# Block-sparse attention and an expert layer on one core: another order of the tiles, and whole rows' scores in quarters of TensorE

## The chip, the core and the metric

The kernel runs on one core of a Trainium2 chip. The metric is the time of one execution on the device, in microseconds (us). Each core has TensorE (PE, matrix products into PSUM), VectorE (DVE), ScalarE (ACT), GpSimd (POOL), and SyncE (SP), which here only issues transfers. Transfers (DMA) are also issued from POOL's queue. Every engine works through its own instructions in the order in which they were written out, and waits for others by semaphores.

## The reference

Attention over 4 batches, 8 heads, 768 positions and head size 64, in blocks of 32 positions, followed by an expert layer on the 3072 tokens:

```python
scores = scale * np.matmul(q, k.transpose(0, 1, 3, 2))
mask = np.abs(blk_i - blk_j) <= window                      # window = 1
mask = mask | (blk_i == 0) | (blk_j == 0) | (blk_i == n_blocks - 1) | (blk_j == n_blocks - 1)
for qb in range(n_blocks):                                  # 24 blocks, 3 sampled keys blocks each
    for kb in sampled_blocks[qb]:
        mask[qb * block:(qb + 1) * block, kb * block:(kb + 1) * block] = True
scores = np.where(mask, scores, -1000000000.0)
attn = exp(scores - max); attn = attn / (sum(attn) + 1e-09)
x = (attn @ v), heads side by side: [3072, 512]
h = np.maximum(x @ w_in, 0.0)                               # [512, 2048]
out = h * h @ w_out                                         # [2048, 512]
```

So a row of an inner block attends to at most eight blocks: the first and the last one, three around itself and three sampled ones. The rows of the first and the last block of a batch attend to all 24 blocks; these are called whole rows.

## The kernel before, in words

**Tiles and chunks.** A tile is 128 positions (4 blocks) of one batch; there are 6 per batch and 24 in all. `order` (line 163) lists them as tile 0 to 5 of batch 0, then of batch 1, and so on. Three tiles make a chunk (`UC`), so there are 8 chunks and two per batch. The attention of a chunk is done ahead of its expert pass. `moe(c)` (line 842) is the expert pass of chunk c: it turns the three tiles' outputs on PE (`turn`, line 765, tile `xt`, split into a high and a low part `xh`, `xl`), then goes through 16 blocks of the hidden layer, each with 12 products (`hidden`, `ph`, line 788) and, two blocks later, its products with the output weights (`project`, `po`, lines 816 and 826).

**Half tiles.** The class `Half` does the inner rows of one tile for four heads. Scores go to two PSUM banks in pieces of 64 rows by 32 columns of PE's array, eight places at once (line 374). The maxima are taken by DVE, the exps by ACT, the transposes by PE in the first two chunks (`turn`, line 437) and by ACT moves and a DVE transpose later (`turn_blocks`), and then come the values (line 459) and the division (`norm`).

**Whole rows.** The class `Whole` does one pair of heads of a batch. The queries of both heads, of the first and of the last block lie in one 128 x 128 operand `QG`, padded with zeros, so that one product with 128 rows and 128 columns gives the scores of both heads against 16 blocks, and a second one against 8 (line 546). Two banks hold them. There are four such units per batch. The first batch's exps are turned on PE (line 584), the others' by moves and a DVE transpose. In `units` (line 629) the whole rows belong to the even chunks (`wholes = [] if c % 2 else ...`): chunk 0 starts with four of them, and then its six half tiles follow.

**Order of the work.** The class `Stream` writes the order out: each unit is a generator, started at a set step and resumed after the lags in `LAG`, `LAG_1` (chunk 1) and `LAG_0` (chunk 0). Before the first expert pass only attention runs (the first stage); from then on each step of an expert pass, 96 to a pass, lets one step of the attention of the next chunk go in between. The score tiles of both kinds and `ph` share five PSUM banks (`SBUFS`), and three more hold the sums of `po`, and in the first stage the turned exps and the values.

**Loads in the first stage.** Keys `kn` and, for whole rows, the values of a batch in natural order (`vn`) come on POOL's queue. On SP's queue come `QG`, q, the static V blocks (first and last), the window V blocks of tile 0 (line 304), and the sampled V blocks: for each of the three tiles 12 transfers with an address from a register (line 317). Windows of tiles 1 and 2 are copied from `vn` by POOL, ACT and DVE (`copy_window`, line 217), the static blocks by ACT (`copy_static`, line 209). Sampled keys are copied by POOL (`copy_keys`, line 263), the fixed keys by POOL (line 284). The weights come as 64-bit numbers on POOL's queue and are cut to 32 bits by ACT and DVE (`cut`, lines 708 to 720); `cut_next` does one step of that, and in the first stage it is called from step 30 on, every 5 steps. Weight blocks named in `SINGLE` are kept as one part and split in each pass (lines 754 and 755), the others are split once.

Of the kernel before, what the change touches and what calls it, by code (L numbers as in the profile page):

```python
# [2 lines left out]

# [53 lines left out]
SINGLE = (1, 2, 3, 5, 6, 7, 9, 10, 11, 12, 13, 14, 15)  # L57
# [21 lines left out]
MOVES_0 = 22  # L79


FIXED_0 = 7
ON_ACT = 12
KEYS_N = 2
# [3 lines left out]
WO_LOW = 3  # L88
# [8 lines left out]
def tile_block_sparse_attention_moe(ctx: ExitStack, tc, kd, knd, qd, qgd, vd, vnd, samp, const, wcat, out):  # L97
# [27 lines left out]
    def indices():  # L125

        n = NBLK * NRAND
        si = rot.tile([1, 2 * n], I32, tag="r", name="si", bufs=2)
        nc.sync.dma_start(si, samp)
        rows = rot.tile([1, 6 * n], F32, tag="ct", name="rows", bufs=2)  # L130
# [25 lines left out]
    QG = one.tile([P, NPAIR, P], F32, name="QG")  # L156
# [6 lines left out]
    order = [(b, t) for b in range(B) for t in range(NT)]  # L163
# [47 lines left out]
    def copy_window(k, i, j, n, copy):  # L211

        b, t = order[k]
        blk = centre(NJ * t + j) - 1 + n
        assert 0 < blk < NBLK - 1
        r = blk % NJ * BLK
        copy(V[k][1][(1 + n) * BLK : (2 + n) * BLK, i, j], st["vn", b, i][r : r + BLK, blk // NJ])

    def load_vn(b, hf, eng=nc.sync, own=None):

        vn = (own or rot).tile([P, NT, HW // 2], F32, tag="vn", name=f"vn{b}_{hf}", bufs=1)
        eng.dma_start(vn.rearrange("p t c -> p (t c)"), vnd[b, hf])
        st["vn", b, hf] = vn
# [15 lines left out]
    def load_q(b, t, eng=nc.sync, own=None):  # L239
        q = (own or rot).tile([P, NJ, NPAIR, BLK], F32, tag="q", name=f"q{b}_{t}", bufs=1 if own else 2)  # L240
        n = NJ * NPAIR * BLK
        eng.dma_start(q.rearrange("p a b c -> p (a b c)"), qd[b, :, t * n : (t + 1) * n])
        st["q", b, t] = q
# [9 lines left out]
    def copy_keys(b, t, own=None):  # L253

        vals = sampled(t, 0, POOL)
        kg = keys_of(b, t, own)
        for u in range(2):
            if t < UC:
                static_keys(b, t, u, nc.gpsimd.tensor_copy)
# [20 lines left out]
    def static_keys(b, t, u, copy=nc.scalar.copy):  # L280
# [3 lines left out]
        copy(dst, src.broadcast_to(list(dst.shape)))  # L284

# [38 lines left out]
    class Half:  # L324
# [34 lines left out]
        def scores(self):  # L359
            b, t, u = self.b, self.t, self.u  # L360
            q, kg, kn = st["q", b, t], st["kg", b, t], st["kn", b, u]
            self.sb = [bank(f"s{self.name}_{e}") for e in range(2)]
# [35 lines left out]
        def next_keys(self):  # L398

            b, t = order[min(self.k + self.u, len(order) - 1)]  # L400
            if b > 0 and t < 2:
# [79 lines left out]
        def loads(self, step):  # L481

            k = order.index((self.b, self.t))
            if step == 0 and self.t == NT - 1 and self.b + 1 < B:
                eng = nc.gpsimd if self.b == 0 else nc.sync
                load_keys(self.b + 1, self.u, eng)
                if self.u == 0:
                    load_whole(self.b + 1, eng)
                    load_vn(self.b + 1, 0, eng)
# [11 lines left out]
            if step == 2 and k not in range(1, UC) and n < len(order):  # L501
                if self.t == NT - 1:
                    load_static(n, self.u)
# [3 lines left out]
    class Whole:  # L507
# [4 lines left out]
        def __init__(self, b, pr):  # L512
            self.b, self.pr = b, pr
            self.name = f"{b}_{pr}"

        def run(self, bank, lag):
            self.scores()
            yield lag["s"]
            self.maxima()
            yield lag["x"]  # L520
            self.exps()
            yield lag["t"]
            if self.b > 0:
                yield from self.move()
                yield lag["w0"]
                self.turn_blocks()
                yield lag["w"]
            else:
                pt = self.turn(bank)
                yield lag["c"]  # L530
                self.copies(pt)
                yield lag["v0"]
            po = self.values(bank)
            if self.pr == 1 and self.b > 0:
                load_vn(self.b, 1)
# [470 lines left out]
```

## Time and profile before

| what | value |
|---|---|
| time, median of the runs | 759.31 us |
| lowest and highest run | 759.08 and 762.59 us |
| the profiled execution, its time | 760.55 us |
| the profiled execution, its span | 758.8 us |
| mean granted clock of TensorE | 0.992 |
| PE, ACT, POOL, DVE busy | 97%, 71%, 66%, 66% |
| transferred | 97.45 MB, mean 128 GB/s |

The span goes from the first to the last instruction; the time also holds what lies around it. The slices of the page divide the span into 40 equal parts and give each engine's busy share in tenths. In the groups each row is a line of the kernel, an engine and an operation; "xh,wi 128*128 128x384" means an array form of 128 rows by 128 columns and a moving operand of 384 columns. A 32-bit product that isn't of the rounded kind is recorded as two instructions, so the scores of one old unit are "x4". In a timeline row come the start, the length, engine, line, operation, the tiles (out<-in), the shape, the count and, in brackets, how long the engine stood idle before it and for whom.

### The profile page before, as it was taken

The numbers are of one execution on the slowest core, as the hardware profiler recorded it, in microseconds if no ns is written. First come the engines' busy times: TensorE is split into PE (matmuls) and PEld (weight loads), VectorE is DVE, ScalarE is ACT, GpSimd is POOL, SyncE is SP. The second block draws the span as 40 slices with busy tenths as digits, with TensorE's granted clock in tenths as the row PEclk, the third lists the DMA queues.
The fourth block names the chain that finished last, engine by engine and source line by source line (L and its number), as shares of the span: only waits on it lengthen the run. The fifth ranks groups of instructions, "written<-read, shape, count | busy, mean of one in ns | idle before, by whom it ended". The sixth has DMA issues, their size and how long they took to land.

```text
span 758.8 us, 26292 instructions
## 1 busy us (share of the span) xinstructions
PE 732.4 (97%) x9832; PEld 612.3 (81%) x9832; DVE 499.8 (66%) x987; ACT 539.7 (71%) x1193; POOL 502.3 (66%) x636
## 2 busy tenths in 40 slices
PE   4879999999999999999999999999999999999997
PEld 2656776668888888888888888887888888888986
DVE  5785785658785756667777575666868666645452
ACT  5896877798876876789786767679876776733222
POOL 6963844227776675757767567666876575777885
PEclk9799999999999999999999999999999999999999
DMA  8776799544543536544434344655344352201001
GB/s 283 224 215 172 228 264 344 130 117 131 140 114 93 146 86 176 153 109 128 113 105 106 101 126 109 221 120 140 79 124 118 75 143 64 51 1 44 1 1 41
DMA packets 92290, 97.45 MB, mean 128 GB/s; under 512 B 14787, under 2 KB 79428, under 8 KB 92164
## 3 DMA queue, kind: packets, MB, share of 16 engines
q1 hardware_dynamic: 86036, 72.41, 37.1%
q0 software_dynamic: 5696, 22.58, 9.2%
q8 instruction: 78, 1.28, 0.7%
q10 hardware_dynamic: 432, 0.79, 0.3%
q14 instruction: 48, 0.39, 0.2%
HBM read 89.43 MB, written 6.29 MB: 126 GB/s over the span
## 4 chain that ended last, share of the span: by engine, by line
PE 85%; ACT 5%; DMA 4%; DVE 4%; issue 1%; SPq 1%; ACTq 0%; POOL 0%; DVEq 0%; POOLq 0%
PE ph L788 33%; PE po L826 30%; PE s L374 7%; PE pv L459 5%; PE po L816 4%; PE g L546 2%; PE pvg L604 2%; DMA V<-in_v_dram 2%; DMA KG<-in_k_dram 1%; PE xt L773 1%; PE pt L437 1%; DVE xl L777 1%; ACT V L209 1%; DMA kn<-in_kn_dram 1%; SPq L317 1%
## 5 line engine op out<-in xcount | busy, mean ns | idle before, releaser
L413 ACT ACTIVATE pm<-p 32x256 f32<-32x256 f32 x576 | 239.2, 415 | 13.2 <-DVE p L391 4.8
L788 PE MATMUL ph<-xh,wi 128*128 128x384 f32 x832 | 237.8, 347 | 0.0
L826 PE MATMUL po<-wo,gh 128*128 128x512 f32 x672 | 213.8, 399 | 0.0
L755 POOL TENSOR_TENSOR wi<-W,wi 128x512 fp32r<-128x512 f32 x104 | 142.3, 1368 | 68.4 <-DVE wi L754 35.2
L806 POOL TENSOR_TENSOR gl<-gf,gh 128x384 fp32r<-128x384 f32 x112 | 117.4, 1048 | 93.0 <-DVE gf L804 80.6
L755 POOL TENSOR_TENSOR wo<-WO,wo 128x512 fp32r<-128x512 f32 x112 | 145.9, 1302 | 49.5 <-DVE wo L754 48.5
L792 ACT ACTIVATE r<-ph 128x384 f32<-128x384 f32 x128 | 63.0, 492 | 161.3 <-PE ph L788 156.1
L804 DVE SCALAR_TENSOR_TENSOR gf<-ph,r 128x384 f32<-128x384 f32 x112 | 62.3, 556 | 150.3 <-ACT r L792 136.4
L788 PEld LDWEIGHTS ph<-xh,wi 128*128 128x128 f32 x832 | 150.4, 188 | 13.4 <-issue 7.4
L826 PEld LDWEIGHTS po<-wo,gh 128*128 128x128 f32 x672 | 123.5, 188 | 23.0 <-issue 2.8
L788 PE MATMUL ph<-xl,wi 128*128 128x384 f32 x416 | 141.4, 340 | 0.0
L826 PE MATMUL po<-wo,gl 128*128 128x512 f32 x336 | 133.2, 396 | 0.0
L754 DVE CAST wo<-WO 128x512 fp32r<-128x512 f32 x112 | 84.4, 753 | 0.0
L788 PEld LDWEIGHTS ph<-xl,wi 128*128 128x128 f32 x416 | 78.2, 188 | 6.9 <-issue 2.9
L826 PEld LDWEIGHTS po<-wo,gl 128*128 128x128 f32 x336 | 63.1, 188 | 15.7 <-POOL gl L806 1.0
L385 DVE TENSOR_REDUCE m<-s 128x2 f32<-128x512 f32 x96 | 61.6, 683 | 11.2 <-PE s L374 10.9
L799 ACT ACTIVATE gh<-r 128x384 fp32r<-128x384 f32 x112 | 59.0, 526 | 9.3 <-ACT r L792 0.4
L459 PEld LDWEIGHTS pv<-V,pT 128*32 128x32 f32 x3072 | 47.7, 110 | 19.8 <-issue 9.5
L459 PE MATMUL pv<-V,pT 128*32 128x65 f32 x3072 | 56.2, 223 | 5.0 <-ACT pT L446 4.8
L788 PE MATMUL ph<-xh,WI 128*128 128x384 f32 x192 | 54.4, 344 | 0.8 <-ACT xh L776 0.8
L374 PE MATMUL s<-KG,q 64*32 64x160 f32 x1536 | 51.2, 305 | 1.4 <-issue 1.0
L418 DVE STREAM_TRANSPOSE pT<-pm 128x1024 f32<-128x1024 f32 x36 | 44.6, 1239 | 4.9 <-ACT pm L413 4.7
(85 smaller groups left out, 933.0 us busy)
## 6 DMA issues: line engine op xcount, KB each, us to landing
craw<-in_w_dram POOLq DMA_DIRECT2D x32, 512.0 KB, 5.9
V<-in_v_dram SPq DMA_DIRECT2D x504, 32.5 KB, 1.8
KG<-in_k_dram SPq DMA_DIRECT2D x216, 64.0 KB, 2.0
V<-in_v_dram SPq DMA_DIRECT2D x28, 390.0 KB, 4.5
q<-in_q_dram SPq DMA_DIRECT2D x24, 256.0 KB, 3.0
out_dram<-ot SPq DMA_DIRECT2D x21, 256.0 KB, 2.5
V<-in_v_dram SPq DMA_DIRECT2D x16, 292.5 KB, 4.2
vn<-in_vn_dram SPq DMA_DIRECT2D x5, 780.0 KB, 6.4
```

What stands on the lines that cost most here:

```text
L374: nc.tensor.matmul(self.sb[e][j * BLK : (j + 1) * BLK, i * NSLOT + a : i * NSLOT + z], q[r, j, pr, :], k, start=True, stop=True,)
L385: nc.vector.tensor_reduce(m[:, e], self.sb[e].rearrange("p (i c) -> p i c", i=2), axis=AX, op=ALU.max)
L413: nc.scalar.activation(p[a * BLK : (a + 1) * BLK, j], x[j * BLK : (j + 1) * BLK, :, a], AF.Exp, scale=SCALE)
L459: nc.tensor.matmul(po[j * BLK : (j + 1) * BLK, h * VW : (h + 1) * VW], self.pT[:, j, 2 * e + i, c], v[:, self.u, j, hv : hv + VW], start=( ...
L754: nc.vector.tensor_copy(w[:, 0], src)
L755: nc.gpsimd.tensor_tensor(w[:, 1], src, w[:, 0], op=ALU.subtract)
L788: nc.tensor.matmul(ph[:, :TOK], w, x, start=(i == 0), stop=(i == len(steps) - 1))
L792: nc.scalar.activation(r, ph[:, :TOK], AF.Relu)
L799: nc.scalar.activation(gh, r, AF.Square)
L804: nc.vector.scalar_tensor_tensor(gf, ph[:, :TOK], 0.0, r, op0=ALU.max, op1=ALU.mult)
L806: nc.gpsimd.tensor_tensor(gl, gf, gh, op=ALU.subtract)
L826: nc.tensor.matmul(acc[c][u], g[:, at], w[:, k], start=(f == 0 and i == 0), stop=(f == NF - 1 and i == 2))
```

## The change

1. **Order.** `order` becomes tile 1, 2, 3, 4, 5, 0 of each batch. The blocks with whole rows lie in tiles 0 and 5, so both are now in the second chunk of a batch, and `units` gives the whole rows to the odd chunks. Chunk 0 has half tiles only; the whole rows of batch 0 come with chunk 1, whose attention lies in the first expert pass. Output rows are addressed by tile.
2. **Whole rows' scores.** `QG` loses its zeros and is half as large. A `Whole` now does two pairs of heads at once. For each of the two spans of keys it makes four products of 64 rows by 64 columns (two heads of a pair, two pairs), each in another quarter of the array. Each head of the pairs has its own rows object (`Rows`), with two banks, so a score step holds four. The rest (maxima, exps, turning, values, norm) is done for each `Rows` as it was for a unit before, with other lags, and the exps have buffers of their own (`pg`).
3. **First stage.** Windows of all three tiles are loaded, those of tiles 1 and 2 of the order on POOL's queue; `vn` and `QG` come last on SP; q of the second and third tile comes on POOL's queue. Static V copies go from ACT to DVE, fixed keys from POOL to ACT. The weight loads are issued between the key copies. Half tiles start every 4 steps, `cut_next` is called from step 13 on, every 7 steps, and the turning of each tile (`turn_tile`) is put into the stage as soon as the tile is done.
4. **Room.** Weight block 4 joins `SINGLE`, and three buffers become smaller or fewer.

The diff's core:

```diff
-SINGLE = (1, 2, 3, 5, 6, 7, 9, 10, 11, 12, 13, 14, 15)
+SINGLE = (1, 2, 3, 4, 5, 6, 7, 9, 10, 11, 12, 13, 14, 15)
-EARLY = 23
+EARLY = 21
-LAG = {"s": 0, "e": 4, "v": 11, "x": 4, "t": 4, "c": 0, "v0": 13, "w0": 4, "w": 16, "n": -1}
+LAG = {"s": 0, "e": 4, "v": 11, "x": 4, "t": 4, "c": 0, "v0": 13, "g": 0, "n": -1}
+LAG.update({("w0", 0): 0, ("w", 0): 16, ("w0", 1): 0, ("w", 1): 8})
-STEP_0 = 5
-STEP_1, FIRST_1 = 12, 0
-LAG_1 = {**LAG, "v": 10, "x": 3, "t": 6, "v0": 5, "n": 0}
-LAG_0 = {"s": 2, "x": 2, "t": 3, "c": 2, "v0": 2, "n": 2}
-CUT_0 = (30, 5)
+STEP_0 = 4
+STEP_1, FIRST_1 = 12, 2
+G_1 = 6
+TURN_0 = (16, 1)
+LOADS_0 = (0, 1, 4, 8, 12)
+OTHERS_0 = (3, 4, 5, 6, 16, 16)
+LAG_1 = {**LAG, "v": 10, "x": 2, "t": 7, "v0": 6, "g": 5, "n": 0}
+LAG_1.update({("w0", 0): 0, ("w", 0): 4, ("w0", 1): 3, ("w", 1): 4})
+LAG_0 = {"s": 1, "x": 2, "t": 2, "c": 1, "v0": 6, "n": 1}
+CUT_0 = (13, 7)
...
-    order = [(b, t) for b in range(B) for t in range(NT)]
+    order = [(b, t % NT) for b in range(B) for t in range(1, NT + 1)]
...
+    class Whole:
+        def __init__(self, b, u):
+            self.b, self.u = b, u
+            self.rows = [Rows(b, u, e) for e in range(2)]
+        def run(self, bank, lag):
+            self.scores()
+            yield lag["s"]
+            for r in self.rows:
+                r.maxima()
+            yield lag["x"]
+            for r in self.rows:
+                r.exps()
+            yield lag["g"]
+            if self.b > 0:
+                for r in self.rows:
+                    yield from r.move()
+            for e, r in enumerate(self.rows):
+                yield lag["w0", e]
+                if self.b > 0:
+                    r.turn_blocks()
+                else:
+                    pt = r.turn(bank)
+                    yield lag["c"]
+                    r.copies(pt)
+                yield lag["w", e]
+                po = r.values(bank)
...
+        def scores(self):
+            kn = st["kn", self.b, self.u]
...
+            for i, n in enumerate(Rows.n):
+                for r in self.rows:
+                    r.sg.append(bank(f"g{r.name}_{i}"))
+                for a in range(2):
+                    for r in self.rows:
+                        at = slice(r.e * D, (r.e + 1) * D)
+                        nc.tensor.matmul(
+                            r.sg[i][a * 2 * BLK : (a + 1) * 2 * BLK, :n],
+                            QG[at, 2 * self.u + a],
+                            kn[at, 16 * i : 16 * i + n // BLK, a, :],
...
-        wholes = [] if c % 2 else [Whole(c // 2, pr) for pr in range(NPAIR)]
+        wholes = [] if c % 2 == 0 else [Whole(c // 2, u) for u in range(2)]
...
+            both += [(2 * i * STEP_1 + FIRST_1 + G_1, u) for i, u in enumerate(wholes)]
...
-        both += [(at + i * STEP + G_AT, u) for i, u in enumerate(wholes)]
+        both += [(at + 2 * i * STEP + G_AT, u) for i, u in enumerate(wholes)]
...
     load_keys(0, 0, nc.gpsimd)
-    load_whole(0)
-    load_q(0, 0)
+    load_keys(0, 1, nc.gpsimd)
+    load_q(*order[0])
+    load_window(0, 0)
     load_static(0, 0)
...
     load_sampled(0, 0, nc.sync, SP)
+    load_q(*order[1], nc.gpsimd)
+    load_q(*order[2], nc.gpsimd, "x", 5)
+    others = [
+        lambda: load_window(1, 0, nc.gpsimd),
+        lambda: load_sampled(1, 0, nc.sync, SP),
+        lambda: load_window(2, 1, nc.gpsimd),
+        lambda: load_sampled(2, 1, nc.sync, SP),
+        lambda: load_whole(0),
+        lambda: load_vn(0, 0),
+    ]
+    for i, _ in enumerate(chain(copy_keys(*order[0]), copy_keys(*order[1]), copy_keys(*order[2], begin))):
+        for at, f in chain(zip(LOADS_0, [cut_next] * AHEAD), zip(OTHERS_0, others)):
+            if at == i:
+                f()
...
+    turns = [(2 * STEP_0 * i + STEP_0 + TURN_0[0], i) for i in range(UC)]
...
-            f(*at, nc.scalar.copy)
-        if now >= MOVES_0 and moves:
-            f, *at = moves.pop(0)
             f(*at, nc.vector.tensor_copy)
```

More of the change, by code (lines that the diff above doesn't have):

```diff
@@ L2 @@
 from contextlib import ExitStack, suppress
+from itertools import chain
 import numpy as np
@@ L154, in indices @@
         return idx
-    QG = one.tile([P, NPAIR, P], F32, name="QG")
+    QG = one.tile([P, NPAIR, 2 * BLK], F32, name="QG")
     V = {0: [one.tile([P, 2, NJ, HW // 2], F32, name=f"V{c}") for c in range(2)]}
@@ L209, in copy_static, with load_vn @@
         copy(dst, src.broadcast_to(list(dst.shape)))
[L211 to L221, printed above, removed]
+    def load_vn(b, hf, eng=nc.sync):
+        vn = rot.tile([P, NT, HW // 2], F32, tag="vn", name=f"vn{b}_{hf}", bufs=1)
         eng.dma_start(vn.rearrange("p t c -> p (t c)"), vnd[b, hf])
@@ L237, in sampled, with load_q @@
         )[1]
-    def load_q(b, t, eng=nc.sync, own=None):
-        q = (own or rot).tile([P, NJ, NPAIR, BLK], F32, tag="q", name=f"q{b}_{t}", bufs=1 if own else 2)
+    def load_q(b, t, eng=nc.sync, tag="q", bufs=2):
+        q = rot.tile([P, NJ, NPAIR, BLK], F32, tag=tag, name=f"q{b}_{t}", bufs=bufs)
         n = NJ * NPAIR * BLK
@@ L398, in next_keys @@
         def next_keys(self):
-            b, t = order[min(self.k + self.u, len(order) - 1)]
-            if b > 0 and t < 2:
+            k = min(self.k + self.u, len(order) - 1)
+            b, t = order[k]
+            if b > 0 and k % NT < 2:
                 static_keys(b, t, 1 - self.u)
@@ L483, in loads @@
             k = order.index((self.b, self.t))
-            if step == 0 and self.t == NT - 1 and self.b + 1 < B:
+            if step == 0 and self.t == order[-1][1] and self.b + 1 < B:
                 eng = nc.gpsimd if self.b == 0 else nc.sync
@@ L505, in loads, with __init__ @@
                 load_sampled(n, self.u, nc.sync, SP)
-    class Whole:
+    class Rows:
         n = (16 * BLK, 8 * BLK)
[L512 to L535, printed above, removed]
-            if lag["n"] >= 0:
-                yield lag["n"]
-            self.norm(po)
-        def scores(self):
-            b, pr = self.b, self.pr
-            kn = st["kn", b, pr // 2]
-            self.sg = [bank(f"g{self.name}_{i}") for i in range(2)]
-            for i, n in enumerate(self.n):
-                k0 = 16 * i
-                nc.tensor.matmul(
-                    self.sg[i][:, :n], QG[:, pr], kn[:, k0 : k0 + n // BLK, pr % 2, :], start=True, stop=True
-                )
+        def __init__(self, b, u, e):
+            self.b, self.u, self.e = b, u, e
+            self.name = f"{b}_{u}{e}"
         def maxima(self):
-            m = self.m = rot.tile([P, 2], F32, tag="mg", name=f"mg{self.name}", bufs=2)
+            m = self.m = rot.tile([P, 2], F32, tag="mg", name=f"mg{self.name}", bufs=4)
             for i, n in enumerate(self.n):
@@ L686, in whole_block @@
             return WO[f]
-        return W1[f] if f in SINGLE else rot.tile([P, DM], F32, tag="ct", name=f"ct{f}", bufs=2)
+        return W1[f] if f in SINGLE else rot.tile([P, DM], F32, tag="ct", name=f"ct{f}", bufs=1)
     def cut_load(f, part):
@@ L965 @@
     vn = np.concatenate([vb[:, V_STATIC : V_STATIC + 1], vb[:, 1 : NBLK - 1], vb[:, V_STATIC + 1 :]], axis=1)
[L968 to L971 removed]
+    qg = pairs(q).reshape(B, P, NBLK, NPAIR, BLK)[:, :, [0, NBLK - 1]].transpose(0, 1, 3, 2, 4)
     kp = pairs(k)
```

120 lines of the change are left out of this document (60 added, 60 removed).

## The prediction

> **What bounds the kernel now.** I read the page first: busy time, the slices and the chain that ended last.
>
> ```profile
> PE 732.4 (97%) x9832; PEld 612.3 (81%) x9832; DVE 499.8 (66%) x987; ACT 539.7 (71%) x1193; POOL 502.3 (66%) x636
> PE   4879999999999999999999999999999999999997
> PE 85%; ACT 5%; DMA 4%; DVE 4%; issue 1%; SPq 1%; ACTq 0%; POOL 0%; DVEq 0%; POOLq 0%
> ```
>
> TensorE (PE) is busy in 97% of the span, and outside the first three of the 40 slices (19 us each) it has no room. So a change can gain in two ways only: end the first stage earlier, or give PE less to do after it. The same stages by windows (columns: stretch, its length, busy of PE, weight loads, DVE, ACT, POOL, granted clock, DMA share, GB/s):
>
> ```profile
> 27.00:30.00 3.00, 0.96 (x35) 0.64 (x36) 2.84 (x9) 2.94 (x9) 2.88 (x10) 1.00 1.04 337
> 30.00:33.00 3.00, 2.43 (x21) 1.98 (x20) 2.79 (x10) 1.23 (x3) 3.00 (x16) 0.50 0.84 192
> 33.00:36.00 3.00, 3.00 (x105) 2.37 (x108) 1.99 (x7) 2.77 (x7) 3.00 (x15) 0.50 0.45 128
> 45.00:57.00 12.00, 8.81 (x318) 7.20 (x317) 9.98 (x21) 12.00 (x27) 8.70 (x26) 1.00 0.81 213
> 65.00:155.00 90.00, 88.61 (x1132) 61.71 (x1130) 61.64 (x104) 72.65 (x142) 43.33 (x69) 1.00 0.78 223
> 160.00:245.00 85.00, 85.00 (x1278) 70.72 (x1277) 62.84 (x131) 67.95 (x159) 59.52 (x66) 1.00 0.48 119
> ```
>
> The end of the first stage is bound by ScalarE (ACT: 12.00 of 12.00 us between 45 and 57), its middle by transfers (DMA share 1.04 at 27 to 30). After 65 us PE is the bound. The timeline of PE gives the places that the sum needs:
>
> ```profile
> 6.61 4.26 PE L546 MATMUL g<-kn,QG 128*128 128x512 f32 x8 [6.61 <-DMA kn<-in_kn_dram]
> 22.63 0.57 PE L374 MATMUL s<-kn,q 64*32 64x96 f32 x16
> 31.15 1.97 PE L437 MATMUL pt<-ident,p 128*128 128x128 f32 x8
> 50.06 1.09 PE L437 MATMUL pt<-ident,p 128*128 128x128 f32 x8
> 56.03 1.38 PE L459 MATMUL pv<-V,pT 128*32 128x65 f32 x64 [0.97 <-ACT pT L446]
> 57.34 1.53 PE L773 MATMUL xt<-ident,x 128*128 128x128 f32 x12
> 59.64 0.44 PE L788 MATMUL ph<-xh,WI 128*128 128x384 f32 x1 [0.78 <-ACT xh L776]
> 60.59 0.44 PE L788 MATMUL ph<-xl,WI 128*128 128x384 f32 x1 [0.50 <-DVE xl L777]
> 61.30 0.40 PE L374 MATMUL s<-kn,q 64*32 64x96 f32 x16
> 62.44 0.44 PE L788 MATMUL ph<-xl,WI 128*128 128x384 f32 x1
> ```
>
> Whole rows take PE from 6.61, the first half tile starts at 22.63, the last values end at 56.03 + 1.38 = 57.4, and the expert's matmuls run without a break from 62.44.
>
> **A. The first stage.** Gone from it: four whole units (scores, maxima, exps, transposes, values), 48 window copies, two cut steps. ACT also loses the six static copies (to DVE) and gets the six static key copies (from POOL). So ACT falls behind no longer; what is late next is the sampled V blocks. They are 36 transfers on SP's queue, before and after, and no value matmul of a tile starts until its 12 have landed:
>
> ```profile
> 3.57 2.22 SPq L304 DMA_DIRECT2D V<-in_v_dram  x4
> 8.21 25.50 SPq L317 DMA_DIRECT2D V<-in_v_dram  x24
> 22.31 5.90 SPq L317 DMA_DIRECT2D V<-in_v_dram  x8
> 33.77 0.58 SPq L242 DMA_DIRECT2D q<-in_q_dram  x1
> 35.36 10.22 SPq L317 DMA_DIRECT2D V<-in_v_dram  x12
> V<-in_v_dram SPq DMA_DIRECT2D x38, 65.0 KB, 4.9
> DMA to landing us min/median/max: 1.6/1.9/9.8
> ```
>
> Before, 24 took 25.50 us and the last 12 took 10.22, with 35.36 - 34.35 = 1.0 us of register loads between. Undisturbed, eight took 5.90, or 0.76 from one to the next (seven steps and one issue of some 0.57). After the change SP has two window transfers in front instead of four (half of 2.22) and one q load instead of two, so the first can go at about 7.2. From there the 36 end between 7.2 + 36 x 0.76 + 2 x 1.0 = 36.6 (all undisturbed, two register loads) and 7.2 + 25.5 + 10.2 + 1.0 = 43.9 (as before). Against the fast end: POOL's queue now carries two q tiles, four windows of 390 KB and five weight blocks in the same 25 us, where it had two vn tiles and the five blocks, and the DMA engines were full (share 1.04) already. I take 41.5, two thirds of the way to the old pace. Landing costs 1.9 (median of the run) to 4.9 (median of these in the first 75 us); I take 3.0, so the last block is there at 44.5. Then two value steps of 1.38 follow: 47.3. New here is that PE has nothing to do for some 6 us before them. In the trace a stretch with 0.96 of 3 us busy is followed by a granted clock of 0.50 up to 36 us, and the eight transposes take 1.97 there against 1.09 at 50.06, 1.8 times as long. At half clock the two value steps take 5.0 instead of 2.8. I take 1.0 of the 2.2 as lost: the last values end at 48.3, a gain of 57.4 - 48.3 = **9.1** (bounds 57.4 - 36.6 - 1.9 - 2.8 = 16.1 and 57.4 - 43.9 - 4.9 - 5.0 = 3.6).
>
> The Trainium skill, "TensorE: Matmul & The Clock Gate", part 1 (the HAM clock gate), says that an idle window of about 3.4 us puts the clock to half and that it takes as long of steady work to lift it. The 0.50 in two rows agrees. By this rule all 2.2 us would be lost, and the estimate would be 1.2 us later than mine.
>
> **B. Into the expert.** Eight of the 12 transposes xt move ahead of the last values; the last tile's four, one ACT copy and one subtraction stay behind them. Before, from 57.4 to 62.44 were 5.0 us, in which PE also did 1.14 us of scores (61.30 to 62.44) and some 0.7 of ph: 3.2 for the passage, with three tiles to copy. The first ph that waited for xh came 2.2 us after 57.4, the first that waited for xl 3.2. With one tile left I take 2.8, between the two. Gain **0.4** (bounds 0 and 1.0).
>
> **C. PE's work after that.** Whole rows of batch 0 now lie in the expert's first pass, where nothing covers them. The rows for their price, all with PE full:
>
> ```profile
> 24.83 0.87 PE L584 MATMUL ptg<-ident,pg 128*128 128x128 f32 x6
> 110.26 0.40 PE L374 MATMUL s<-kn,q 64*32 64x96 f32 x16
> 111.40 1.13 PE L816 MATMUL po<-WO,gp 128*128 128x512 f32 x2
> 181.30 0.89 PE L604 MATMUL pvg<-vn,pTg 128*32 128x65 f32 x48
> 182.12 0.62 PE L788 MATMUL ph<-xh,wi 128*128 128x384 f32 x2
> 182.58 0.34 PE L788 MATMUL ph<-xl,wi 128*128 128x384 f32 x1
> 192.32 1.45 PE L546 MATMUL g<-kn,QG 128*128 128x512 f32 x4
> 193.42 0.53 PE L788 MATMUL ph<-xl,wi 128*128 128x384 f32 x1
> 193.79 0.51 PE L788 MATMUL ph<-xh,wi 128*128 128x384 f32 x2
> ```
>
> A ph matmul passes every 0.17 us (the pairs of 0.51 are two that overlap). Scores of one old unit: 193.79 - 192.32 less one ph = 1.30. Values: 182.58 - 181.30 less two ph = 0.93. Transposes of a batch-0 row set: 0.87. The new scores are not in this trace. The half tile's scores are the nearest row: 64 rows by 32 columns of the array, eight places at once, 16 products of 96 and 16 of 160 columns, or 512 full columns; they take 111.40 - 110.26 = 1.14, where 512 columns at the old unit's rate (1.30 for 768) are 0.87. So eight places do run side by side, with 0.27 for changing the array's form and back. Four quarters of 768 columns then take 1.30 + 0.27 = 1.57 for two pairs; bounds 1.30 (no change of form seen) and 2 x 1.30 + 0.27 = 2.87 (only two side by side).
>
> Before, batches 1 to 3 had 12 x (1.30 + 0.93) = 26.8 in the PE-bound part. After: 8 x 1.57 + 16 x 0.93 + 4 x 0.87 = 12.6 + 14.9 + 3.5 = 30.9. A loss of **4.2** (bounds 2.0 and 14.6).
>
> Costed at nothing are batch 0's maxima, exps, copies and norms and two cut steps, which now fall into 65 to 155 us, and the split of weight block 4 in each of the eight passes. Rows for them and for the banks below:
>
> ```profile
> L755 POOL TENSOR_TENSOR wi<-W,wi 128x512 fp32r<-128x512 f32 x104 | 142.3, 1368 | 68.4 <-DVE wi L754 35.2 <-ACT wi L752 31.3 <-PE ph L788 1.2
> L754 DVE CAST wi<-W 128x512 fp32r<-128x512 f32 x91 | 47.3, 520 | 0.0
> 176.43 1.45 PE L546 MATMUL g<-kn,QG 128*128 128x512 f32 x4
> 179.35 1.01 DVE L553 TENSOR_REDUCE mg<-g 128x1 f32<-128x512 f32 x2
> 182.94 1.05 ACT L562 ACTIVATE pg<-g,mg 128x512 f32<-128x512 f32 x2
> ```
>
> Maxima are 4 x 1.01 on DVE, exps 4 x 1.05 on ACT; with as much again or twice for the rest, both still fit under PE, since ACT is busy 72.65 of those 90 us and DVE 61.64. Block 4 is 8 x 1.37 on POOL and 8 x 0.52 on DVE, under PE as well, which is full; with that cover gone, at most 11 + 4. The output rows and loads in another order hang on SP, off the path.
>
> **D. Banks.** One score step now takes four of the five PSUM banks at once, not two, until both rows' exps are done. In the last rows a unit's banks are held from 176.43 to 182.94 + 1.05 = 184.0, 7.6 us; the next half tile's two banks are wanted 7 of 16 loop steps later, and 16 steps are 192.32 - 176.43 = 15.9, so at 183.4. PE would stand 0.6 us or not at all, and DVE has another 1.01 of maxima and more in front of the second row's exps. Behind a waiting score matmul stands all of PE's queue. I take 0.1 for each of eight (between none and 1.5): **0.8**.
>
> Sum: -9.1 - 0.4 + 4.2 + 0.8 = -4.5. The profiled execution took 760.55 with a span of 758.8, so 756.0 for that one; it lies 1.2 above the median of the runs shown (759.31), and against that median the forecast is **754.8 us**.
>
> **Rivals.** (1) The sampled blocks go at their undisturbed pace and the clock stays up: A gains 16.1, D nothing, and -16.1 - 0.4 + 4.2 = -12.3 gives 747.0. For it: eight at 0.76 in the middle of a full DMA stretch. Against it: the 25.50 for 24.
> (2) The loads end as late as they did (3.6 gained): -3.6 - 0.4 + 4.2 + 0.8 = +1.0, 760.3, no change. For it: 36 issues behind a fuller POOL queue. Against it: fewer transfers ahead on SP.
> (3) On the other side, the banks: the exps of the second row come so late that each score step holds up the next half tile by 1.5 us. 8 x 1.5 = 12, less the 0.8 counted: 754.8 + 11.2 = 766.0. It is slower than before from 0.7 us a step on. For it: the 0.6 us above; against it: a unit with both rows lies 32 steps from the next. The Trainium skill, "TensorEngine Tiling (Array Packing)", Gotcha 1 (PSUM Pressure), warns that row tiles need more banks; no run here shows it yet.
> (4) The quarters don't run side by side: 2.87 a step, 8 x 1.30 = 10.4 more, 765.2. Against it: the 1.14 of eight places.
>
> **How the numbers follow.** Chances: the forecast 0.36 (its own range 751 to 758), (1) 0.22, (2) 0.22, (3) 0.09, (4) 0.05, anything else 0.06. A measurement of this kernel can just tell 0.5%, or 3.8 us, from no change, so faster means under 755.5: 0.28 of the forecast, all of (1) and 0.02 are 0.52. No change: 0.08 of the forecast, 0.17 of (2), 0.03: 0.28. Slower: the rest of (2), (3), (4), 0.01: 0.20. The range of 8 in 10 goes from (1) to a little over (2): 746 to 762.
>
> **What would show it.** The last values of chunk 0 should end near 48, waiting for sampled V rather than for ACT's copies; after them a granted clock of 0.50 if the clock's step is right. A score step of two pairs should fill about 1.6 us of PE in the passes, and no half tile's scores should wait for an exp of whole rows. PE's idle time after 60 us should stay under 3 us. It would be wrong if values end after 53 or before 44, or if PE waits for cut weights in the first pass, because ACT or DVE is fuller there than I sum.

## The result and the profile after

The changed kernel takes 770.51 us (median; 766.34 to 771.65), the kernel before 759.63 us beside it (759.08 to 762.59). The ratio is 1.0125 with a 95% interval of 1.0079 to 1.0171: slower by 1.25%, where 754.8 us and a gain were forecast. (The ratios here and below come from means of runs taken side by side, so they can lie up to 0.4% off the quotient of the medians.) The profiled execution took 770.36 us with a span of 768.6, 9.8 us more than the span before. The rows of this section are of that one execution; over the four runs the mean granted clock goes from 0.981 to 0.995, so waits and half-clock stretches differ somewhat from one execution to the next.

The page of the changed kernel: busy time, PE's slices, and the chain that ended last.

```profile
PE 730.5 (95%) x9896; PEld 607.4 (79%) x9896; DVE 525.0 (68%) x988; ACT 525.0 (68%) x1169; POOL 506.8 (66%) x629
PE   2678999999999999999999999899999999999997
PE 81%; DVE 8%; ACT 5%; issue 3%; POOL 2%; POOLq 0%; DMA 0%; ACTq 0%; DVEq 0%
```

PE is busy 1.9 us less than before, so the work did shrink a little. The time was lost in waiting: 38 us without PE in place of 26, and "issue" and DVE take 11% of the chain where they had 5%. The slices put it into the first four of them (to 77 us) and the 26th (480 to 500 us).

To say where, I cut the span at the last transpose `xt` of a pass, which every kernel here has. These rows are the timeline of PE, first before (its first such row, at 57.34, stands in the prediction), then after:

```profile
157.36 1.47 PE L773 MATMUL xt<-ident,x 128*128 128x128 f32 x12
681.66 1.47 PE L773 MATMUL xt<-ident,x 128*128 128x128 f32 x12
```

```profile
54.67 0.44 PE L805 MATMUL xt<-ident,x 128*128 128x128 f32 x2 [1.07 <-DVE x L481]
166.33 1.47 PE L805 MATMUL xt<-ident,x 128*128 128x128 f32 x12
691.21 1.47 PE L805 MATMUL xt<-ident,x 128*128 128x128 f32 x12
```

| stretch | before | after | difference | forecast |
|---|---|---|---|---|
| to the end of the first stage's xt | 58.9 | 55.1 | -3.8 | -9.5 (A and B) |
| first expert pass, to the next xt | 100.0 | 112.7 | +12.7 | +10.3 (C: the rows of batch 0) |
| six passes more | 524.3 | 524.9 | +0.6 | -5.4 (rest of C, and D) |
| to the end of the span | 75.7 | 75.9 | +0.3 | 0 |

The forecast column is the prediction's sum laid over the same stretches: 2 x 1.57 + 4 x 0.93 + 4 x 0.87 = 10.3, and 6 x 1.57 + 12 x 0.93 - 26.8 + 0.8 = -5.4. So three stretches failed, by 5.7, 2.4 and 6.0 us.

**First stage.** The timeline of POOL, and below it the waits of PE up to 62 us (total, times, longest) and SP's sampled loads:

```profile
9.92 0.71 POOL L304 DMA_DIRECT2D V<-in_v_dram  x1
15.37 0.69 POOL L304 DMA_DIRECT2D V<-in_v_dram  x1 [4.74 <-issue]
16.06 0.58 POOL L262 COPY KG<-kn 128x64 f32 x3
22.29 0.68 POOL L304 DMA_DIRECT2D V<-in_v_dram  x1 [2.32 <-issue]
```

```profile
PE s L375 <- POOL KG L262: 10.9, 5, 4.8
PE s L375 <- issue: 2.6, 1, 2.6
PE pv L461 <- issue: 1.5, 1, 1.5
PE pt L439 <- issue: 1.1, 1, 1.1
```

```profile
6.25 37.27 SPq L317 DMA_DIRECT2D V<-in_v_dram  x36
```

POOL issues the windows of the second and third tile itself. Between the two issues of a pair it stands, for 4.74 and 2.32 us, and the key copies of the coming half tiles stand in the same queue behind them. PE waits 10.9 us for key copies, 4.8 and 3.7 of them right behind these two stalls. The last of SP's sampled loads, on which the prediction put the bound, is issued by 43.5, and in this whole stage no value matmul waits for V.

Then PE's own timeline:

```profile
44.55 0.49 PE L375 MATMUL s<-KG,q 64*32 64x160 f32 x10 [2.60 <-issue]
45.46 1.82 PE L439 MATMUL pt<-ident,p 128*128 128x128 f32 x8
47.22 1.92 PE L461 MATMUL pv<-V,pT 128*32 128x65 f32 x64
52.11 1.12 PE L461 MATMUL pv<-V,pT 128*32 128x65 f32 x64
59.22 0.40 PE L375 MATMUL s<-kn,q 64*32 64x96 f32 x16
60.36 0.61 PE L820 MATMUL ph<-xh,WI 128*128 128x384 f32 x2
66.17 3.58 PE L848 MATMUL po<-WO,gp 128*128 128x512 f32 x4 [2.76 <-DVE WO L746]
69.68 1.52 PE L641 MATMUL g<-kn,QG 64*64 64x512 f32 x16
71.13 1.13 PE L848 MATMUL po<-WO,gp 128*128 128x512 f32 x2
484.74 0.30 PE L375 MATMUL s<-kn,q 64*32 64x96 f32 x6 [2.18 <-issue]
```

From 25.65 on PE is never again short of data for long, and still the last values end only at 52.11 + 1.12 = 53.2. In between lie three pauses of 1.5, 1.1 and 2.6 us which no semaphore explains ("issue"), each in the middle of a group of short matmuls; the last section says what they go with. After the longest the clock is halved. Windows of the changed kernel: round that pause, behind it, in the passage to the expert, behind the wait for WO, and behind a pause of the same kind at 484 us (columns as in the prediction: PE, weight loads, DVE, ACT, POOL, granted clock, DMA share, GB/s):

```profile
41.50:45.40 3.90, 1.29 (x36) 0.72 (x20) 0.59 (x2) 1.72 (x4) 0.00 (x0) 1.00 0.95 261
45.50:48.80 3.30, 3.30 (x70) 2.97 (x71) 1.64 (x4) 2.65 (x6) 0.00 (x0) 0.51 0.90 310
55.90:59.10 3.20, 2.98 (x8) 2.26 (x8) 3.17 (x4) 0.62 (x1) 3.20 (x10) 0.50 0.99 291
66.10:69.30 3.20, 3.13 (x4) 1.17 (x4) 2.51 (x4) 3.17 (x8) 1.68 (x5) 0.50 0.48 152
486.00:489.20 3.20, 3.20 (x9) 2.64 (x9) 2.02 (x4) 2.46 (x6) 1.01 (x1) 0.50 0.24 55
```

Each of these stalls of 2.2 to 2.8 us is followed by some 3.4 us at half clock, which costs up to 1.7 us more; one such stretch (55.9 to 59.1) follows the shorter waits of the passage.

**After the first stage.** Waits of PE behind 62 us, after and then before:

```profile
PE s L375 <- issue: 3.0, 3, 2.2
PE po L848 <- DVE WO L746: 2.8, 1, 2.8
PE pvg L569 <- DVE gf L836: 1.8, 3, 0.6
PE po L858 <- POOL gl L838: 1.2, 4, 0.3
```

```profile
PE s L374 <- ACT pg L562: 1.5, 2, 0.8
PE s L374 <- issue: 1.0, 1, 1.0
```

Before, PE waited 2.7 us in 700; after, 9.1 us with the smallest, and the clock takes another 3.4.

### The profile page after: what moved, and what is told of

The parts are those of the page before. It is cut to its first block, busy times and chain, and to the rows that moved or that the text cites. A ratio compares the mean times of both kernels' runs of the same rounds, so it can differ in the third digit from the quotient of the medians.

```text
span 768.6 us, 26464 instructions
## 1 busy us (share of the span) xinstructions
PE 730.5 (95%) x9896; PEld 607.4 (79%) x9896; DVE 525.0 (68%) x988; ACT 525.0 (68%) x1169; POOL 506.8 (66%) x629
## 3 DMA queue, kind: packets, MB, share of 16 engines
q8 instruction: 79, 1.29, 0.7%
## 4 chain that ended last, share of the span: by engine, by line
PE 81%; DVE 8%; ACT 5%; issue 3%; POOL 2%; POOLq 0%; DMA 0%; ACTq 0%; DVEq 0%
PE ph L820 31%; PE po L858 26%; PE s L375 7%; PE pv L461 6%; PE po L848 5%; PE pvg L569 2%; PE pt L439 2%; ACT pm L415 1%; ACT pgm L537 1%; DVE m L386 1%; DVE p L392 1%; DVE gf L836 1%; DVE mg L520 1%; DVE wo L780 1%; PE xt L805 1%
## 5 line engine op out<-in xcount | busy, mean ns | idle before, releaser
L820 PE MATMUL ph<-xh,wi 128*128 128x384 f32 x896 | 255.1, 346 | 0.0
L781 POOL TENSOR_TENSOR wi<-W,wi 128x512 fp32r<-128x512 f32 x112 | 153.2, 1368 | 86.6 <-DVE wi L780 47.4
L820 PEld LDWEIGHTS ph<-xh,wi 128*128 128x128 f32 x896 | 162.8, 188 | 12.6 <-issue 7.7
L838 POOL TENSOR_TENSOR gl<-gf,gh 128x384 fp32r<-128x384 f32 x112 | 122.9, 1097 | 68.0 <-DVE gf L836 63.8
L820 PE MATMUL ph<-xl,wi 128*128 128x384 f32 x448 | 150.9, 337 | 0.0
L780 DVE CAST wo<-WO 128x512 fp32r<-128x512 f32 x112 | 90.2, 805 | 0.1
L820 PEld LDWEIGHTS ph<-xl,wi 128*128 128x128 f32 x448 | 84.2, 188 | 6.4 <-issue 2.9
L375 PE MATMUL s<-KG,q 64*32 64x160 f32 x1536 | 56.2, 310 | 14.5 <-POOL KG L262 10.9
L831 ACT ACTIVATE gh<-r 128x384 fp32r<-128x384 f32 x112 | 58.9, 526 | 10.2 <-ACT r L824 0.4
L780 DVE CAST wi<-W 128x512 fp32r<-128x512 f32 x98 | 63.2, 645 | 0.0
L461 PEld LDWEIGHTS pv<-V,pT 128*32 128x32 f32 x3072 | 49.4, 110 | 15.8 <-issue 11.6
L848 PE MATMUL po<-WO,gp 128*128 128x512 f32 x96 | 49.1, 627 | 2.8 <-DVE WO L746 2.8
```

What stands on the lines that cost most here:

```text
L375: nc.tensor.matmul(self.sb[e][j * BLK : (j + 1) * BLK, i * NSLOT + a : i * NSLOT + z], q[r, j, pr, :], k, start=True, stop=True,)
L461: nc.tensor.matmul(po[j * BLK : (j + 1) * BLK, h * VW : (h + 1) * VW], self.pT[:, j, 2 * e + i, c], v[:, self.u, j, hv : hv + VW], start=( ...
L780: nc.vector.tensor_copy(w[:, 0], src)
L781: nc.gpsimd.tensor_tensor(w[:, 1], src, w[:, 0], op=ALU.subtract)
L820: nc.tensor.matmul(ph[:, :TOK], w, x, start=(i == 0), stop=(i == len(steps) - 1))
L838: nc.gpsimd.tensor_tensor(gl, gf, gh, op=ALU.subtract)
```

## The experiments

Each is compared with runs of the kernel before on the same chip. "After" is the changed kernel. Of its variants only runs 4, 14 and 15 lie clear of its own interval (1.0079 to 1.0171); for the others the times alone show no gain or loss against it, and what is said of them rests on the rows of one profiled execution each.

**1 and 2. The windows on another queue.** In the changed kernel, one line for each tile:

```diff
-        lambda: load_window(1, 0, nc.gpsimd),
+        lambda: load_window(1, 0, nc.scalar),      # run 2: nc.sync; the third tile the same
```

> The changed kernel, but the window V blocks of the second and third tile are issued from ACT's queue instead of POOL's, where they stand between the key copies. Theory 1 (POOL's queue: it stood 4.7 and 2.3 us behind the second transfer of each pair, and the key copies of the second half tile behind it): the second half tile's scores end near 15 us instead of 25.5, the last values of chunk 0 end near 49 instead of 53.2, when the last sampled V blocks are there; 4 us less than the changed kernel, about 766. Theory 2 (transfers are the bound whoever issues them): the last values end at 53 as before, no change, 770.

> The same, but on SP's queue, where each pair of windows goes ahead of the tile's 12 sampled blocks. Theory 1: POOL's copies are free as in the run with ACT's queue, but 24 sampled blocks stand behind some 2 us of issues each, so the last values end 1 to 3 us later than there, near 51; about 768. Theory 2: no change, 770.

On ACT's queue: 774.1 us, ratio 1.016 (1.0109 to 1.0212). POOL was free, but ACT now stood behind the same transfers, and PE waited 7.7 us for its exps and 11.2 for V; the last values ended at 59.0, not near 49 as theory 1 had it. ACT's timeline and PE's waits:

```profile
11.34 7.48 ACTq L304 DMA_DIRECT2D V<-in_v_dram  x2
18.86 2.18 ACT L283 COPY KG<-kn 128x512 f32<-128x512 f32 x4 [8.37 <-DMA V<-in_v_dram]
```

```profile
PE pv L461 <- DMA V<-in_v_dram: 11.2, 6, 4.1
PE pt L439 <- ACT p L425: 7.7, 1, 7.7
```

On SP's queue: 767.29 us, ratio 1.0088 (1.0061 to 1.0116). The third half tile's scores start at 15.4, not 27.5, so the queue of POOL is shown as the cause of that wait. But the last values end at 51.75, only 1.5 us earlier. PE's timeline says why:

```profile
21.11 1.78 PE L439 MATMUL pt<-ident,p 128*128 128x128 f32 x8 [3.79 <-ACT p L425]
25.89 0.40 PE L461 MATMUL pv<-V,pT 128*32 128x65 f32 x2 [2.64 <-DMA V<-in_v_dram]
42.75 0.77 PE L375 MATMUL s<-KG,q 64*32 64x160 f32 x10 [3.38 <-issue]
```

ACT's exps and the sampled V of the first tile are late next (four of the 64 value matmuls ran at 22.8, ahead of that wait, so a tile's values don't all wait for its 12 loads, as the prediction had it). The pause within the scores of the last half tile is still there, longer than it was. So the 12 us of the queue were worth 1.5.

**3 and 7. Cut steps earlier**, alone and with the windows on SP.

```diff
-CUT_0 = (13, 7)
+CUT_0 = (9, 5)
```

> The changed kernel with the cut steps of the first stage from step 9 on, every 5 steps, six of them instead of four. Theory 1 (PE's wait of 2.8 us for output weights at 63.4 us and the half clock of 3.4 us after it come from the two cut steps that were moved behind): both go, 4 us less, about 766. Theory 2 (the cut steps lengthen the first stage by as much, since ACT and DVE then do them before the last tile's norm and split): within 1 us of the changed kernel, 770.

> The changed kernel with the windows of the second and third tile on SP's queue and six early cut steps together. Theory 1 (the two lost times are separate: POOL's blocked queue 3 us, cut weights 2.4 us): 5.4 us less than the changed kernel, about 765. Theory 2 (the stage is then bound by the sampled V blocks, which the windows on SP push back, so that the cuts fill only waiting time, and the wait moves to the whole rows' exps in the first pass): like the run with SP alone, 767.

Alone: 767.94 us, ratio 1.0069 (1.0038 to 1.01). The wait for WO is gone; it had come from cut steps that ran too late, not from the whole rows (it stands in run 4 too, which has none there). In its place, 9 us further on, stands one of the same size, for exps of whole rows:

```profile
PE pt L439 <- ACT pg L528: 2.6, 1, 2.6
```

With the windows on SP: 769.82 us, 1.0114 (1.0081 to 1.0146). The two changes don't add up to a gain: the profiled execution has that wait, a pause of 2.0 us at 486, and a wait of 2.7 us for the third tile's sampled V:

```profile
53.58 1.72 PE L461 MATMUL pv<-V,pT 128*32 128x65 f32 x50 [2.75 <-DMA V<-in_v_dram]
```

So here the sampled loads are late next, as theory 2 had it.

**4. Whole rows of batch 0 left out**, their output rows set to zero.

```diff
+        if c == 1:
+            wholes = [Skipped(0)]
```

> The changed kernel without the whole rows of batch 0: their 64 rows of the attention's output are set to zero, so the first and the last block of batch 0 come out otherwise. Theory 1 (their cost in the first expert pass is PE's own work, two score steps of 1.45, four transposes of 0.87, four values of 0.93): 10 us less, about 760. Theory 2 (their work on ACT, DVE and in the banks stops PE as well): 14 us less or more, 756 or under.

758.09 us, ratio 0.9969 (0.9942 to 0.9996), 12.4 below after, with those rows not computed. The first pass takes 102.4 us in place of 112.7, so these rows cost 10.3 us there; the prediction's terms say 10.3. The wait for WO is the same 2.8, and the pause at 484 us isn't there, though nothing near that place was edited.

**5, 9 and 10. The quarters in the kernel before**, with batch 0's rows where they were: with the exps in the shared buffers (5); with the changed kernel's room and exp buffers (9); and with the moves of a row set two loop steps apart (10). **8** is the room alone.

```diff
-        wholes = [] if c % 2 else [Whole(c // 2, pr) for pr in range(NPAIR)]
+        wholes = [] if c % 2 else [Whole(c // 2, u) for u in range(2)]     # 5, 9, 10, with Rows
-SINGLE = (1, 2, 3, 5,
+SINGLE = (1, 2, 3, 4, 5,                                                  # 8, 9, 10
-                        yield 1
+                        yield 2                                            # 10
```

> The kernel before with the whole rows' scores of two pairs in quarters of TensorE and nothing else of the change: tiles 0 to 5, whole rows in the even chunks, the first stage as it was. Theory 1 (the quarters save PE 2 x 1.30 - 1.45 for two pairs, in six units of batches 1 to 3 where PE is the bound): 6.9 us less than before, about 752.5; the loss of the whole change then lies in the order and the first stage alone. Theory 2 (four banks for a score step hold up the half tiles by what is saved): within 2 us of before, 759. Theory 3 (the banks cost more): slower than before.

> The kernel before with only the room made: weight block 4 kept as one part and split in each pass, one buffer less for cut blocks and for the indices. Theory 1 (that work is under PE): no change, 759 within 1 us. Theory 2 (the splits keep PE waiting): 2 to 5 us more.

> The quarters alone on the kernel before, as in the run before last, but with the same room, so that the exps of whole rows have buffers of their own instead of taking those of the split weights. Theory 1 (in that run the exps' buffers kept the weights' splits, and so PE, waiting; the quarters themselves save 2.3 us in each of three batches): 6.9 less than before, about 752.5, and PE waits for no split. Theory 2 (four banks at once or the crowded half tiles eat the saving): 757 to 762. Theory 3 (what made the run 16 us slower was not the buffers): 770 or more again.

> The kernel before with the new score step and batch 0's rows left where they were (as in the run with quarters and room, 782.4 us), but the 16 moves of a row set are laid two loop steps apart, not one. Theory 1, a burst of moves on ScalarE and GpSimd, because the two row sets of a score step are moved at once, puts ScalarE behind, and the banks are held for that: waits of PE for ScalarE's exps and GpSimd's gelu fall by half or more of their 19 us, 765 to 773 us. Theory 2, the four of five banks taken in one step are what PE waits for, whatever the pace of the moves: 778 to 784 us, and the waits for exps of whole rows stay.

Room alone: 760.55 us, ratio 1.0018 (0.9991 to 1.0046), no change, so the split of block 4 costs nothing that can be measured. Quarters: 775.1 (1.018, 1.014 to 1.0219), 782.4 (1.0281, 1.0243 to 1.0318) and 781.17 (1.0277, 1.0251 to 1.0303). The waits of PE after 62 us, of run 9 and then of run 10:

```profile
PE po L849 <- POOL gl L829: 4.2, 9, 0.6
PE s L376 <- ACT pg L529: 2.1, 1, 2.1
```

```profile
PE s L376 <- ACT pg L529: 6.3, 4, 2.1
PE po L849 <- POOL gl L829: 1.8, 4, 0.5
```

This is rival (3), half tiles whose scores wait for exps of whole rows, in a kernel where the four banks are taken with the changed lags, but without the changed starting steps. Laying the moves apart cut the waits for POOL and raised those for ACT, with no gain: theory 1, the burst, falls, and the time lies where theory 2, the banks, had it. That two row sets at once always cost this falls in run 13. What in the older order makes it so is left open; these runs carry the changed kernel's lags inside the older starting steps, so they don't test the quarters by themselves.

**6 and 11. Smaller shifts of the whole rows in after**: values three loop steps earlier; moves two steps apart.

```diff
-LAG.update({("w0", 0): 0, ("w", 0): 16, ("w0", 1): 0, ("w", 1): 8})
+LAG.update({("w0", 0): 0, ("w", 0): 13, ("w0", 1): 0, ("w", 1): 8})       # 6
-                        yield 1
+                        yield 2                                            # 11
```

> The changed kernel with the first row object's values of whole rows three steps earlier, so that they no longer stand directly before the values and scores of half tiles. Theory 1 (PE's pauses that nothing released, 2.2 us at 482 us, come when some 350 short instructions stand together and the next 16 KB of its instructions are not there yet; the clock then drops to half for 3.4 us): the pause and the drop at 482 us go, 3 to 4 us less, about 766.5. Theory 2 (the pause has to do with the place in the program or with other transfers, not with the crowd of short instructions): a pause of 1 us or more somewhere between 440 and 520 us stays, 770.

> The changed kernel with the moves of a row set two loop steps apart. If bursts of moves cost the changed kernel anything behind its first pass, its waits for banks after 170 us (1.8 of values of whole rows, 1.2 of output, some 3 in all) go: 767 to 769 us. If they don't: 770 to 772 us, or a microsecond or two more since each row set's values come later and its copies are held longer. In both cases the two crowds of short matmuls with their pauses may shift, which moves the time by 4 us either way.

Run 6: 775.98 us, ratio 1.0182 (1.0128 to 1.0236). The pause at 484 is gone, with its crowd of matmuls drawn apart. But values of whole rows now meet a bank that `gf` still reads, three times 2.7 us, each followed by half clock (the waits, and the window behind the third one):

```profile
PE pvg L569 <- DVE gf L836: 8.1, 3, 2.7
```

```profile
632.70:635.90 3.20, 3.20 (x53) 2.65 (x50) 1.65 (x8) 3.12 (x8) 1.70 (x2) 0.50 0.02 5
```

8.1 - 1.8 for the waits and 3 x 1.7 for the clock, less 3.9 for the pause that went, is 7.5; the span grew by 6.6. Run 11: 768.3 us, ratio 1.014 (1.0093 to 1.0188). The waits for banks and for POOL's `gl` (3.0 us together) and the pause at 484 (2.2 and 1.7) are gone, yet passes 2 to 7 together are only 3.0 us shorter. PE's idle time in them fell from 5.8 to 2.5 us, with new pauses of up to 0.7; its busy time stayed at 519 although the half clock was gone, and why is open.

**12. Third tile's sampled loads made cheap**, on run 2: six transfers of a fixed block for the 12, which leaves the tile's sampled part out of the result.

```diff
-        lambda: load_sampled(2, 1, nc.sync, SP),
+        lambda: load_fixed(2),
```

> The changed kernel with the windows of the second and third tile on SyncE's queue (as in the run that gave 767.3 us), and the 12 sampled V transfers of the third tile replaced by 6 transfers of a fixed block; the third tile's sampled part is left out of the computation so. If the 12 transfers at SyncE's pace (their issue ended at 47.3 us there) are what the first stage's end waits for: the last values end at 46 to 49 us, not 51.5, and the time is 762 to 765 us. If PE's pause of 3.4 us at 42.8 and ScalarE's copies bound it: the last values end at 50.5 to 52, and the time stays 766 to 768 us.

Last values end at 49.4, 2.3 us earlier than in run 2 and just past what was expected if the 12 transfers are waited for (46 to 49); but the trace gives another reason. In neither run did the third tile's values wait for V. What shrank is the pause, from 3.38 to 1.14:

```profile
41.69 0.49 PE L383 MATMUL s<-KG,q 64*32 64x160 f32 x10 [1.14 <-issue]
```

So the sampled loads weren't what PE waited for in run 2. But they had no slack: the last of them, issued at 46.8, landed at 48.9, while those values ran from 48.78 on; in run 7 they are waited for. The profiled execution took 762.58 us, the four runs 762.58, 764.83, 770.74 and 774.09 (ratio 1.0143, 1.0087 to 1.0198), so the time itself tells nothing apart.

**13 to 15. One row set per score step**, in after (13) and in a version with all small edits (15); 14 is that version with two: windows on SP, early cuts, moves apart, and batch 0's rows 18 steps later.

```diff
-        wholes = [] if c % 2 == 0 else [Whole(c // 2, u) for u in range(2)]
+        wholes = [] if c % 2 == 0 else [Whole(c // 2, u, e) for u in range(2) for e in range(2)]   # 13, 15
-G_1 = 6
+G_1 = 24                                                                                           # 14, 15
```

> The changed kernel, order and layout kept, but each row set has its own score step of two quarters (two row sets 12 loop steps apart in chunk 1, as half tiles are, and as before in the others). Theory 1, the step of two row sets gains what its row in the trace shows (1.45 us for two against 2 x 1.30) and its four banks cost about 3 us: 16 steps of 1.3 in place of 8 of 1.45 are 9.2 us more work for PE, the bank waits of some 3 us go, 775 to 778 us. Theory 2, two row sets at once are what costs the time, as the runs with quarters in the kernel before look: the waits fall by more than the work grows, 762 to 768 us.

> The changed kernel with the four smaller edits at once: windows on SyncE, cut steps from loop step 9 on, moves two steps apart, and whole rows of batch 0 begun 18 loop steps later in the first pass, so that the first pass has its cut blocks ready before. If the waits named are what keeps the changed kernel behind (first stage 1.5, weights in the first pass 2.8 + 1.7, banks 3): 758 to 762 us. If each removed wait is only replaced by the next (as with early cuts alone, 767.9): 766 to 769 us.

> The run before with one row set per score step. By the theory that the step of two row sets gains (1.15 us a step): 7 to 9 us above the run before it in this list. By the theory that two at once cost more in waits: below it, 755 to 760 us.

Run 13: 775.09 us, ratio 1.0177 (1.0109 to 1.0246), as theory 1 had it. The bank waits are gone, and PE is busy through all of its six passes, 525.8 us; in run 11, which has no bank waits either, it is busy 519.4 of 521.9. So in the changed order the step of two row sets saves PE 6.4 us of work in these passes (12 x 1.30 - 6 x 1.45 = 6.9 by the rows), and 3.9 of time. The values' places shift too, so this isn't the step by itself. Runs 14 and 15 took 781.27 (1.0249, 1.0183 to 1.0315) and 785.75 (1.032, 1.0257 to 1.0383): the later rows came with a new stall, shown here for run 14.

```profile
134.37 2.96 PE L641 MATMUL g<-kn,QG 64*64 64x512 f32 x16 [8.63 <-DMA QG<-in_qg_dram]
```

`QG` has one buffer, and a half tile of chunk 1 has batch 1's queries loaded into it (from POOL, issued at 128.97). In after that load is issued at 126.6, behind batch 0's two score steps (69.7 and 100.9). With batch 0's scores 18 steps later it stands ahead of the second of them, the one at 134.37, which therefore waited 8.63 us and was given batch 1's queries; run 15 has the same. So these two runs compute something else, and say little of the small edits together. Less the 8.6 and some 2.3 for the clock behind them (half of the 4.6 us up to 139), run 14 would be near 770, by estimate. None of the versions that do the whole work beats the kernel before.

## Why the prediction was wrong, step by step

Two of the prediction's own signs of being wrong came up: the last values ended after 53, and PE waited for cut weights in the first pass.

**A, first stage: failed, 4.2 us gained in place of 9.1.** The step that failed is "what is late next is the sampled V blocks". POOL's new windows were counted as rivals of SP's transfers, but not as instructions in POOL's own queue with the key copies behind them; run 2 shows that this was what held the third half tile. The forecast's 41.5 for SP's end came out at 43.5, within its bounds, and nothing waited for it. What then set 53.2 are PE's pauses, 1.5 + 1.1 + 2.6 = 5.2 us, and the half clock behind them: transposes 1.82 for 1.09 and values 1.92 for 1.12, 1.5 us. The sampled V stood close behind: the last, issued at 42.6, landed 4.3 us later, at 46.9. With two value steps of 1.38 behind it the stage could hardly have ended before 49.7 (an estimate), so without the pauses the forecast 48.3 would have been missed by little, and for the reason that it gave. As it came, the clock's loss was right in kind (1.0 taken, 1.5 measured); its cause was a pause, not an empty wait for V.

**B, into the expert: failed, 1.4 lost in place of 0.4 gained.** By the prediction's own count: from 53.2 to 60.36, when the ph matmuls go on behind the scores, are 7.1 us, less 1.1 of scores and 1.4 for the eight ph in between: 4.6 for the passage, against 3.2 before. DVE's timeline in after:

```profile
54.53 0.68 DVE L745 SCALAR_TENSOR_TENSOR W<-W,craw 128x512 int32<-128x512 int32 x1
55.95 0.68 DVE L810 TENSOR_TENSOR xl<-xt,xh 128x512 fp32r<-128x512 f32 x1
63.63 0.69 DVE L745 SCALAR_TENSOR_TENSOR WO<-WO,craw 128x512 int32<-128x512 int32 x1 [1.68 <-ACT craw L736]
```

A cut step of DVE lies between the last tile's norm and its `xl`, but PE waited only 0.2 us for `xl`. What was lost is the clock: the eight ph took 2.98 us at half clock (55.9 to 59.1, 0.50) in place of 1.4.

**C, PE's work: right.** The quarters run side by side: 71.13 - 69.68 = 1.45 for two pairs, against 1.57 forecast and 2 x 1.30 before. The rows of batch 0 cost 10.3 as summed. With 1.45 the work after the first stage grows by 3.2, not 4.2.

**Costed at nothing, failed: 4.5 us.** The cut steps in the first pass weren't hidden: PE stood 2.8 us for WO and lost 1.7 to the clock. The reason I had given for such a wait, fuller ACT or DVE, isn't what held it. DVE was fuller in this pass (75% in place of 67%), ACT was not (75% for 78%), and DVE stood idle 1.68 us for ACT's half of the cut (the row at 63.63); run 3 removes the wait by starting earlier. The first pass misses its forecast by 2.4 only: PE stood 4.0 us in it, 1.3 more than before, lost 3.2 to the clock with the passage's share, but did 8.2 us more work and not 10.3. Run 4 puts the rows themselves at 10.3; what got 2 us cheaper beside them isn't traced. The split of block 4 was rightly nothing (run 8).

**D, banks: about the size, but elsewhere.** No score matmul of half tiles waited for an exp of whole rows in after. Values of whole rows waited 1.8 us for a bank that `gf` still read, where before PE waited 1.5 for exps: net 0.3, forecast 0.8. Output matmuls waited another 1.2 for `gl`, an operand that POOL makes, which stands in no term. The Trainium skill, "TensorEngine Tiling (Array Packing)", Gotcha 1, warns of PSUM pressure from row tiles. The trace agrees in kind (1.8), and run 6 shows the price on a worse phase: 8.1.

**In no term: the pause at 484 us**, 2.2 us and 1.7 of clock. Of the 6.0 by which the six passes miss the forecast, it is 3.9, two smaller pauses 0.8, and the waits for banks and `gl` above the forecast 0.8 are 1.9, less the 1.5 of waits for exps that before had. The other 0.9 is PE's work: it was busy 522.8 us in these passes before and 519.1 after, or 5.3 less without the clock's 1.7, where the sum has 6.2 (and 6.9 with 1.45). Why it shrank by less is open.

**Rivals.** Rivals (3) and (4) gave 766.0 and 765.2, on the right side, but by mechanisms that weren't there in after. (3) is real in runs 5, 9 and 10. Nothing was set down for a queue that stands behind its own transfers, nor for PE's pauses.

## What to carry to other kernels

When transfers move to another engine's queue, read what that engine has to do behind them: the 390 KB loads cost POOL 4.7 and 2.3 us of standing still, and the second pair on ACT 7.5. A PE-bound stretch has little to give, and a wait of over 2 us can count nearly twice, by the clock after it; a shift of three loop steps made and removed such waits. Removing one wait in a tight stage is worth what lies between it and the next: 12 us of earlier scores brought 1.5. When a score step or a load is moved, look whether the single buffer that it reads is still the right one (runs 14 and 15).

## What the runs showed that was not expected

**Pauses of PE without a releaser.** They stand in crowds of short matmuls: 1.5, 1.1 and 2.6 us in the first stage, 2.18 at 484.74 behind 148 short matmuls and their weight loads (from 479.91 to 482.24), 3.38 in run 2, and up to 1.7 before the change. They go with the packets of one instruction queue, of which the page of after counts 79 and the stretch from 481 to 486 us has one:

```profile
q8 instruction: 79, 1.29, 0.7%
q8 instruction: 1, 0.02, 1.2%
```

A packet has 16 KB, and there is one to some 250 of PE's matmuls and weight loads (9896 of each; before, 78 for 9832 of each). The one near 484 was read from 482.3 to 483.3, within the pause, and PE went on 1.4 us after its end. In the 17 traces there are 35 pauses of 1.2 us or more that no semaphore explains, and each of the 35 ends 1.2 to 1.6 us after a packet of this queue; by chance one in 25 would (79 times 0.4 us of 769). So PE very likely waits for its own instructions there. The 148 matmuls and their loads are more than a packet in 2.7 us, where a packet lasts 9.7 us on average. But no run tests this by itself, and a crowd alone isn't enough: the pause near 484 stands in runs 1, 2, 3 and 7 (1.94, 1.45, 2.16 and 2.0 us), but not in runs 4 and 12, which leave the order around it as it is. Why the packet comes late in some executions is open.

**The clock falls after less than a full window.** The Trainium skill, "TensorE: Matmul & The Clock Gate", part 1, gives one idle window of about 3.4 us as the condition. Here idle stretches of 2.2 to 2.8 us were enough, with PE busy 1.29 of the 3.90 us from 41.5 to 45.4; the 3.4 us at half clock agree with the page. All changes of the clock in the 17 traces lie on a grid of 3.41 us. Of the grid's stretches at full clock up to PE's last matmul, all 44 with PE busy for under 1.5 us were followed by half clock, of the 39 with 1.5 to 2.1 us 12 were, and of the 3542 with more none. So it counts how a gap lies on the grid: one of 2.42 us in run 10 (50.2 to 52.6) is cut by it at 51.9, leaves PE busy for 1.8 and 2.5 us in the two stretches, and full clock followed.
